# First activations in their own tiles, stored one step sooner; square issued ahead of the subtraction; second output weights kept for two blocks

## Chip, cores and metric

One core of one Trainium2 chip runs the whole program. The metric is device time in microseconds (us) of one execution; the time before is the median of three runs. The parts that matter are TensorE (PE, matrix products; PEld its weight loads), ScalarE (ACT), VectorE (DVE), GpSimd (POOL), SyncE (SP, which here only issues transfers) and the 16 DMA engines.

## The reference

A retention layer, then two MLPs without bias over the same 4608 tokens, all in float32:

```python
ret = (q @ k.T) / 8 * Dmat          # per batch and head, Dmat[i, j] = gamma**(i - j) for i >= j, else 0
x = (ret @ v)                       # heads put side by side: 4608 x 512
h = x @ w_in;  g = h * sigmoid(1.702 * h);  x2 = g @ w_out        # 512 -> 2048 -> 512
h = x2 @ w_in2; g = h - tanh(h);            out = g @ w_out2
```

Each operand of a large product is split into a rounded high part and the rest (two fp32r tiles), and the product is the sum of three passes: high by high, high by low, low by high.

## The kernel before

Tokens lie in 9 blocks of 512 (`NB`), the inner width of 2048 in 16 slices of 128 (`NF`). A **step** s = 16 j + f of the first MLP is `mm_in(s)`: 12 matmuls that give h for block j and slice f, in one PSUM bank. `act_a(s)` makes g from it: ACT takes a tanh into a tile t (L456), DVE makes g in place (L458). `g_store(s)` (L485) sends the tile to DRAM from SP's queue. A **unit** o is the output product of the same numbering: `g_load(o)` brings g back (L504), `act_b(o)` splits it (ACT L509, DVE L510), `wo_load` brings the slice of w_out (L216), and `mm_out` does four parts of 3 matmuls (L526, L528) into four accumulators. After the 16th slice of a block `evac` copies each accumulator to a tile o (ACT L550) and sends it out from ACT's queue (L536).

The order of work on every engine is written out by hand; each engine, and SP's and ACT's transfer queues, go strictly in that order. A tile that is allocated waits until an earlier tile of its tag has been released.

- **Steps 0 to 31** run ahead of all units, beside the retention layer and the decoding of the weights (`dec_a` to `dec_store`, which load raw words L103, use ACT L115, L148 and DVE L113 to L155, and store decoded weights L166, L169).
- **Steps 32 to 79** each carry one unit, o = s - 32 (`LAG`), and every second one a half tile of the retention layer (`attn_step`). Per step SP has in order: the loads of w_out and g for unit o + 2 (`out_loads`), the load of an attention tile, stores of decoded weights, the g store, loads of raw weights. `stores(2)` keeps the two newest steps unstored, so the store issued in step s is that of s - 2. Blocks end with units 15, 31 and 47, in steps 47, 63 and 79.
- **Steps 80 to 143** carry no units (`PAUSE`), but retention until step 126.
- **Tile tags.** `p` has 5 tiles of 128x512: the masked scores of the retention layer (`bat_p`, L326, one in every second step), the t of odd steps, and the four o of an evacuation. `t` has 3 tiles: the t of even steps.
- **The second MLP** starts with one plain block (L677) and goes on with 4 pairs of blocks; for a pair, 7 products of combined operands (`mm_part`, L690) stand for 8, so that a loop step u (32 of them, q = u mod 8) gives four h tiles for `act_2`, between units of the output product. `act_2` does on ACT tanh (L472), square of h (L475), square (L476), relu (L477) and on DVE h - tanh (L474), L479, L480 and a predicated copy (L481). h lies in PSUM in the plain block and in one of four calls per u (L475 with input x); in the other three it lies in SBUF.
- **w_out of the last two blocks** (units 256 to 287): slices 3 to 15 are loaded once each into tiles of the 18 operand tags (`wo_stay`, `xo_tile`, L223), slices 3 to 6 at the end of the last but one u, and 7 to 15 two at a time in the calls of `ready()` in the last u, where the operand tiles become free. Slices 0 to 2 are loaded for each of the two blocks by `wo_load`, like all others.

Of the kernel before, what the change touches and what calls it, by code (L numbers as in the profile page):

```python
# [14 lines left out]
ACTF = mybir.ActivationFunctionType  # L15
# [10 lines left out]
NB = NT // BLK  # L26
KD = DM // P
NF = DFF // P
# [14 lines left out]
PAUSE = 80  # L43
# [5 lines left out]
def kernel(  # L49
# [11 lines left out]
    nc = tc.nc  # L61
# [142 lines left out]
    def wo_load():  # L204
        o = n_w[0]
        n_w[0] += 1
        j, f = divmod(o, NF)
        if j == 0 or j >= 2 * NB or (j >= 2 * NB - 2 and f > 2):
            return
        n_w[1] += 1  # L210
        if second and n_w[1] % 4 == 0:
            t = second["pool"].tile([P, 2, DM], F32R, tag="wos2", name="wos", bufs=1)
        else:
            t = wos_p.tile([P, 2, DM], F32R, tag="wos", name="wos")
        wos[o] = t
        nc.sync.dma_start(out=t.rearrange("p a n -> p (a n)").bitcast(F32), in_=wo_d[int(j >= NB), f])  # L216

    def wo_stay(f):

        if not 2 < f < NF:  # L220
            return
        t = xo_tile()
        nc.sync.dma_start(out=t.rearrange("p a n -> p (a n)").bitcast(F32), in_=wo_d[1, f])  # L223
        for j in (2 * NB - 2, 2 * NB - 1):
            wos[j * NF + f] = t
# [222 lines left out]
    def act_a(s):  # L448

        h = hps.pop(s)  # L450
        if s % 2:
            t = p_p.tile([P, BLK], F32, tag="p", name="t")
        else:
            t = t_p.tile([P, BLK], F32, tag="t", name="t", bufs=3)
        tt[s] = t
        nc.scalar.activation(out=t, in_=h, func=ACTF.Tanh, scale=0.851)  # L456
        copies_out(0)
        nc.vector.scalar_tensor_tensor(out=t, in0=t, scalar=1.0, in1=h, op0=ALU.add, op1=ALU.mult)  # L458
# [3 lines left out]
    def act_2(s, h):  # L462

        tt[s] = t = turn("t")
        sq = t_p.tile([P, BLK], F32, tag="e", name="sq")
        pl = t_p.tile([P, BLK], F32, tag="z", name="pl", bufs=3)
        if not marks:
            marks["t"] = st_p.tile([P, 2, BLK], F32, tag="stg", name="marks", bufs=3)
            marks["n"] = 0
        small = marks["t"][:, marks["n"] % 2]  # L470
        marks["n"] += 1
        nc.scalar.activation(out=t, in_=h, func=ACTF.Tanh)  # L472
        copies_out(0)
        nc.vector.tensor_tensor(out=t, in0=h, in1=t, op=ALU.subtract)  # L474
        nc.scalar.activation(out=sq, in_=h, func=ACTF.Square)  # L475
        nc.scalar.activation(out=pl, in_=sq, func=ACTF.Square, bias=abias)  # L476
        nc.scalar.activation(out=small, in_=sq, func=ACTF.Relu, bias=sbias, scale=-1.0)  # L477

        nc.vector.scalar_tensor_tensor(out=pl, in0=pl, scalar=CB, in1=sq, op0=ALU.add, op1=ALU.mult)  # L479
        nc.vector.scalar_tensor_tensor(out=pl, in0=pl, scalar=C2, in1=h, op0=ALU.mult, op1=ALU.mult)  # L480
        nc.vector.copy_predicated(out=t, mask=small.bitcast(I32), data=pl)  # L481

    def g_store(s):
        gd[s] = dram.tile([P, BLK], F32, tag=f"g{s}", name="gd")
        nc.sync.dma_start(out=gd[s], in_=tt.pop(s))  # L485
# [4 lines left out]
    def turn(what):  # L490

        shape, dt, n = {"t": ([P, BLK], F32, 3), "gl": ([P, BLK], F32, 2), "g": ([P, 2, BLK], F32R, 2)}[what]
        i = turns[what]
        turns[what] += 1
        more = {"t": 3, "gl": 2, "g": 1}[what]
        if second and i % (n + more) >= n:
            return second["pool"].tile(shape, dt, tag=what + "2", name=what, bufs=more)
        if what == "g":
            return g_p.tile(shape, dt, tag="g", name="g")
        return t_p.tile(shape, dt, tag=what, name=what, bufs=n)  # L500
# [31 lines left out]
    def copies_out(keep):  # L532

        while len(copies) > keep:
            dst, o = copies.pop(0)
            nc.scalar.dma_start(out=dst, in_=o)  # L536
# [21 lines left out]
    def out_loads(o):  # L558
        while n_w[0] <= min(o + (3 if second else 2), n_steps - 1):
            wo_load()  # L560
        while n_g[0] <= min(o + (4 if second else 2), n_steps - 1):
            g_load(n_g[0])
            n_g[0] += 1

    def out_split(o):
        while n_b[0] <= min(o + (2 if second else 1), n_steps - 1):
            act_b(n_b[0])
            n_b[0] += 1
# [20 lines left out]
    def xo_tile():  # L589
        tag = xo_tag.pop(0)  # L590
        xo_tag.append(tag)
        if tag == "ws":
            return st_p.tile([P, 2, DM], F32R, tag="ws", name="xo", bufs=2)
        return wts.tile([P, 2, DM], F32R, tag=tag, name="xo")
# [159 lines left out]
    with tc.tile_pool(name="ps_e", bufs=RING - 1, space=bass.MemoryType.PSUM) as ps_e:  # L754
# [11 lines left out]
        for b in range(BPB + 1):  # L766
            if b == 0:
                for bt in range(BPT):
                    at_scale(0, (bt, bt + 1))
                    for i in range(2):  # L770
                        for k in range(2):
                            h = 2 * (2 * bt + k) + i
                            nc.scalar.activation(
                                out=mt_sb[:, bt, i, k], in_=mk_sb, func=ACTF.Copy, scale=jt_sb[:, h:h + 1]
# [51 lines left out]
    def stores(keep):  # L826
        while len(done) > keep:
            g_store(done.pop(0))
# [10 lines left out]
    for s in range(LAG, NB * NF):  # L839
        j, f = divmod(s, NF)  # L840
        o = s - LAG
        if s < PAUSE:
            out_loads(o)
        mm_in(s)
        b = EARLY + BPB + (s - LAG) // 2
        if s % 2 == 0 and b <= TILES * BPT:
            attn_step(b)
            if b == TILES * BPT:
                early_ctx.close()
                second["pool"] = ctx.enter_context(tc.tile_pool(name="second", bufs=1))  # L850
                second["psum"] = ctx.enter_context(tc.tile_pool(name="ps_x", bufs=1, side="right", space=bass.MemoryType.PSUM))
        dec_piece()
        act_a(s)
        if s < PAUSE:
            out_split(o)
        done.append(s)
        stores(2)
        if s < PAUSE:
            some(outs, 4)
        dec_piece(2 if j == 2 else 1)  # L860
        if n_dec[0] >= 3 * (len(chunks) + 2):
            some(prep, 1)
        if j == NB - 1 and f >= 5:
            some(std, 1)
        if j == NB - 1 and f in (8, 11, 14):
            wq_load((f - 8) // 3, True)
# [4 lines left out]
    for i in range(NF):  # L871
        q, half_ = divmod(i, 2)
        s = NB * NF + q + half_ * QS
        h = ps_h.tile([P, BLK], F32, tag="h", name="h")
# [30 lines left out]
    for u in range(pairs * QS):  # L905
        p, q = divmod(u, QS)
        ja = NB + 1 + 2 * p
        a, b = (ja * NF + q, (ja + 1) * NF + q)
        end = p == pairs - 1
        if q == 0:  # L910
            xo.update(new)
            new = {}
            ops = xo_prep(3 + 2 * p, new) if not end else iter(())
        final = q == QS - 1
        stay = iter(range(7, NF)) if end and final else iter(())

        def ready():
            if final:
                some(ops, 1)
                for f in islice(stay, 2):  # L920
                    wo_stay(f)

        n = 4 if final else 3
        x_ps = second["psum"].tile([P, BLK], F32, tag=f"x{u % 2}", name="x")
        y_ps = ps_h.tile([P, BLK], F32, tag="h", name="y")

        mm_part(x_ps, q, 1, True)
        m1 = copied(x_ps, "m1")
        some(outs, n)
        if late:  # L930
            act(*late[0])

        mm_part(y_ps, q, 5, True)
        m5 = copied(y_ps, "m5")
        some(outs, n)
        if late:
            act(*late[1])
        ready()

        mm_part(x_ps, q, 6, False)  # L940
        u2 = copied(x_ps, "u2")
        some(outs, n)
        if u + 1 < pairs * QS:
            wq_load((q + 1) % QS, False)
        ready()

        mm_part(y_ps, q, 3, False)
        h12 = added(y_ps, u2, "h12")
        some(outs, n)
        ready()  # L950

        mm_part(x_ps, q, 7, False)
        h22 = added(x_ps, m5, "h22")
        some(outs, n)
        act(a + QS, h12)
        ready()

        w_ps = second["psum"].tile([P, BLK], F32, tag=f"x{1 - u % 2}", name="w")
        mm_part(w_ps, q, 2, True)
        h11 = added(w_ps, m1, "h11")  # L960
        some(outs, n + final)
        ready()

        mm_part(x_ps, q, 4, False)
        some(outs, 4 + final)
        act(b + QS, h22)
        if not final and q:
            some(ops, 1)
        if end and q == QS - 2:
            for f in range(3, 7):  # L970
                wo_stay(f)
        late = ((a, h11), (b, x_ps))
    for n in late:
        some(outs, 4)
        act(*n)
# [57 lines left out]
```

## Time and profile before

| what | before |
|---|---|
| median of 3 runs (lowest, highest) | 1724.05 us (1722.04, 1724.18) |
| the profiled execution, its own time | 1721.87 us |
| its span, first to last instruction | 1720.1 us |
| PE busy | 1691.1 us (98%) |
| DVE, ACT, POOL busy | 1111.2, 885.1, 113.1 us |
| bytes moved | 497.44 MB, mean 289 GB/s |
| granted TensorE clock, mean | 0.995 of full |

How to read it: PE is busy in nearly all of the span, so its idle time is short and can be listed gap by gap. A gap stands in the timeline in square brackets behind the first instruction after it, with what ended it. The chain of waits follows the last instruction back through what released it. Idle time of the other engines costs nothing unless a PE gap hangs on it. Landing is the time from the issue of a transfer to its end.

### The profile page before, as it was taken

To read this page: it belongs to the slowest core of one execution; us is meant where nothing else is said; L and a number is where in the kernel's file an instruction comes from. 1 tells how busy PE (TensorE), PEld (TensorE's weight loads), DVE (VectorE), ACT (ScalarE), POOL (GpSimd) and SP (SyncE) were. 2 spreads that over 40 slices of the span, in tenths; PEclk is the share of its full clock that TensorE was granted. 3 is DMA by queue.
4 is the path that set the end of the run, shared out by engine and by line. 5 is a ranking of instruction groups with operands and counts; after the bars stand their busy time and mean duration, and the time that the engine had idled before them with its cause. 6 is when DMAs were issued, how large, how long until landed. Compare 5 with 4: busy or idle time off the path is not lost.

```text
span 1720.1 us, 24553 instructions
## 1 busy us (share of the span) xinstructions
PE 1691.1 (98%) x8714; PEld 1383.0 (80%) x8714; DVE 1111.2 (65%) x1806; ACT 885.1 (51%) x1684; POOL 113.1 (7%) x104
## 2 busy tenths in 40 slices
PE   7999999999999999999999999999999999999999
PEld 5788887878877888887888888888888888888777
DVE  6787885656676444457577786677766776666532
ACT  4444442333344433446566576566666665656532
POOL 4011100011002321000000000000000000000000
PEclk9999999999999999999999999999999999999999
DMA  7467779888887777898899899998999999889962
GB/s 265 151 224 248 278 270 317 273 286 281 297 303 275 251 284 250 313 334 293 297 356 315 300 314 332 343 324 278 327 345 315 310 316 310 301 305 327 381 192 86
DMA packets 173866, 497.44 MB, mean 289 GB/s; under 512 B 19632, under 2 KB 20784, under 8 KB 164400
## 3 DMA queue, kind: packets, MB, share of 16 engines
q1 hardware_dynamic: 162800, 476.91, 79.9%
q10 hardware_dynamic: 10944, 18.96, 2.9%
q8 instruction: 69, 1.13, 0.3%
q14 instruction: 53, 0.43, 0.1%
HBM read 363.67 MB, written 132.12 MB: 288 GB/s over the span
## 4 chain that ended last, share of the span: by engine, by line
PE 87%; DMA 5%; DVE 4%; ACT 2%; issue 1%; SPq 0%; ACTq 0%; POOL 0%; DVEq 0%
PE acc L526 21%; PE acc L528 21%; PE h L443 20%; PE x L690 10%; PE y L690 5%; PE w L690 2%; DMA gl<-gd 2%; PE pat L303 2%; PE h L677 2%; DMA x<-o 2%; PE pat L349 1%; PE pat L289 1%; PE pat L318 1%; DVE p L326 1%; DMA at<-in_attn_dram 0%
## 5 line engine op out<-in xcount | busy, mean ns | idle before, releaser
L526 PE MATMUL acc<-g,wos 128*128 128x512 f32 x1536 | 378.0, 394 | 7.3 <-DVE g L510 3.5
L443 PE MATMUL h<-xh,wi 128*128 128x512 f32 x1152 | 374.0, 394 | 2.5 <-ACT xh L363 1.3
L528 PE MATMUL acc<-wos,g 128*128 128x512 f32 x1416 | 344.3, 389 | 3.1 <-DMA wos<-wd 2.5
L526 PEld LDWEIGHTS acc<-g,wos 128*128 128x128 f32 x1536 | 289.3, 189 | 71.8 <-DVE g L510 4.2
L509 ACT ACTIVATE g<-gl 128x512 fp32r<-128x512 f32 x288 | 180.0, 627 | 299.9 <-PE acc L528 150.2
L528 PEld LDWEIGHTS acc<-wos,g 128*128 128x128 f32 x1416 | 265.4, 188 | 59.9 <-ACT marks L477 2.4
L510 DVE TENSOR_TENSOR g<-gl,g 128x512 fp32r<-128x512 f32 x288 | 201.8, 702 | 169.0 <-ACT g L509 167.5
L443 PEld LDWEIGHTS h<-xh,wi 128*128 128x128 f32 x1152 | 216.4, 188 | 53.5 <-issue 5.3
L443 PE MATMUL h<-xl,wi 128*128 128x512 f32 x576 | 224.6, 390 | 0.6 <-DVE xl L364 0.6
L690 PE MATMUL x<-xo,wq 128*128 128x512 f32 x768 | 195.2, 389 | 0.0
L690 PEld LDWEIGHTS x<-xo,wq 128*128 128x128 f32 x768 | 143.9, 188 | 30.8 <-ACT u L896 1.0
L479 DVE SCALAR_TENSOR_TENSOR pl<-pl,sq 128x512 f32<-128x512 f32 x144 | 99.7, 692 | 102.8 <-ACT pl L476 102.4
L458 DVE SCALAR_TENSOR_TENSOR t<-t,h 128x512 f32<-128x512 f32 x144 | 98.4, 685 | 68.4 <-ACT t L456 63.8
L115 ACT ACTIVATE e<-e,ebias 128x512 int32<-128x512 int32 x64 | 46.3, 724 | 180.9 <-DVE e L113 180.9
L443 PEld LDWEIGHTS h<-xl,wi 128*128 128x128 f32 x576 | 108.3, 188 | 23.0 <-DVE xl L364 1.4
L481 DVE COPY_PREDICATED t<-marks,pl 128x512 f32<-128x512 int32 x144 | 109.4, 760 | 15.2 <-ACT xo L597 0.5
L364 DVE TENSOR_TENSOR xl<-pat,xh 128x256 fp32r<-128x256 f32 x61 | 25.8, 423 | 142.0 <-ACT xh L363 139.9
L456 ACT ACTIVATE t<-h 128x512 f32<-128x512 f32 x144 | 84.2, 587 | 50.1 <-PE h L443 49.8
L476 ACT ACTIVATE pl<-sq,abias 128x512 f32<-128x512 f32 x144 | 104.2, 724 | 4.7
L477 ACT ACTIVATE marks<-sq,sbias 128x512 f32<-128x512 f32 x144 | 102.1, 709 | 0.0
L690 PE MATMUL y<-xo,wq 128*128 128x512 f32 x384 | 97.4, 389 | 0.0
L363 ACT ACTIVATE xh<-pat 128x256 fp32r<-128x256 f32 x61 | 23.2, 381 | 136.3 <-PE pat L349 136.3
(89 smaller groups left out, 1957.7 us busy)
## 6 DMA issues: line engine op xcount, KB each, us to landing
wos<-wd SPq DMA_DIRECT2D x246, 512.0 KB, 5.4
gd<-t SPq DMA_DIRECT2D x288, 256.0 KB, 5.4
gl<-gd SPq DMA_DIRECT2D x288, 256.0 KB, 5.2
stg<-in_w_dram SPq DMA_DIRECT2D x64, 512.0 KB, 6.5
at<-in_attn_dram SPq DMA_DIRECT2D x32, 1024.0 KB, 6.0
wq<-wq SPq DMA_DIRECT2D x32, 1024.0 KB, 7.6
wq<-wq SPq DMA_DIRECT2D x32, 768.0 KB, 9.3
wd<-ws SPq DMA_DIRECT2D x32, 512.0 KB, 4.5
```

What stands on the lines that cost most here:

```text
L443: nc.tensor.matmul(h, lhsT=win[f][:, a, k], rhs=xs[b][:, k], start=(n == 0), stop=(n == 3 * KD - 1))
L456: nc.scalar.activation(out=t, in_=h, func=ACTF.Tanh, scale=0.851)
L458: nc.vector.scalar_tensor_tensor(out=t, in0=t, scalar=1.0, in1=h, op0=ALU.add, op1=ALU.mult)
L476: nc.scalar.activation(out=pl, in_=sq, func=ACTF.Square, bias=abias)
L477: nc.scalar.activation(out=small, in_=sq, func=ACTF.Relu, bias=sbias, scale=-1.0)
L479: nc.vector.scalar_tensor_tensor(out=pl, in0=pl, scalar=CB, in1=sq, op0=ALU.add, op1=ALU.mult)
L481: nc.vector.copy_predicated(out=t, mask=small.bitcast(I32), data=pl)
L509: nc.scalar.activation(out=g[:, 0], in_=t, func=ACTF.Copy)
L510: nc.vector.tensor_tensor(out=g[:, 1], in0=t, in1=g[:, 0].bitcast(F32), op=ALU.subtract)
L526: nc.tensor.matmul(acc[m], lhsT=wo[:, a, c], rhs=g[:, b], start=first, stop=last)
L528: nc.tensor.matmul(acc[m], lhsT=g[:, a, c], rhs=wo[:, b], start=first, stop=last)
L690: nc.tensor.matmul(ps, lhsT=wq[q][t][:, o // 2, o % 2 * 2 + k, a], rhs=xo[i][k][:, b], start=first and n == 0, stop=n == 5, skip_group_che ...
```

## The change

In the steps 32 to 84 the t of odd steps comes from the tag `t` like that of even ones, and in steps 32 to 79 only the newest step stays unstored. In `act_2` the square is issued ahead of the subtraction. All 16 slices of the second w_out are loaded once for the last two blocks: slices 0 to 3 at the end of the last but one u, 4 to 15 in the last one, in which `ready()` is called once more.

```diff
@@ wo_load
-        if j == 0 or j >= 2 * NB or (j >= 2 * NB - 2 and f > 2):
+        if j == 0 or j >= 2 * NB - 2:
             return
@@ wo_stay
-        if not 2 < f < NF:
-            return
         t = xo_tile()
@@ act_a
-        if s % 2:
+        if s % 2 and not 2 * NF <= s <= PAUSE + 4:
             t = p_p.tile([P, BLK], F32, tag="p", name="t")
         else:
             t = t_p.tile([P, BLK], F32, tag="t", name="t", bufs=3)
@@ act_2
         nc.scalar.activation(out=t, in_=h, func=ACTF.Tanh)
         copies_out(0)
+        nc.scalar.activation(out=sq, in_=h, func=ACTF.Square)
         nc.vector.tensor_tensor(out=t, in0=h, in1=t, op=ALU.subtract)
-        nc.scalar.activation(out=sq, in_=h, func=ACTF.Square)
@@ steps 32 to 143
-        stores(2)
+        stores(1 if s < PAUSE else 2)
@@ pairs of blocks
-        stay = iter(range(7, NF)) if end and final else iter(())
+        stay = iter(range(4, NF)) if end and final else iter(())
@@ end of a loop step u
         if end and q == QS - 2:
-            for f in range(3, 7):
+            for f in range(4):
                 wo_stay(f)
         late = ((a, h11), (b, x_ps))
+        ready()
```

## Rows read from the trace of the kernel before

**Rows 1.** The page, part 1: busy time, share and instructions of engines.
```profile
PE 1691.1 (98%) x8714; PEld 1383.0 (80%) x8714; DVE 1111.2 (65%) x1806; ACT 885.1 (51%) x1684; POOL 113.1 (7%) x104
```

**Rows 2.** Timeline of PE: start, duration, what, and the gap before it.
```profile
276.81 5.06 PE L526 MATMUL acc<-g,wos 128*128 128x512 f32 x11 [3.17 <-DVE g L510]
...
384.44 0.49 PE L526 MATMUL acc<-g,wos 128*128 128x512 f32 x1 [1.94 <-ACT g L509]
385.25 4.24 PE L526 MATMUL acc<-g,wos 128*128 128x512 f32 x11 [0.31 <-DVE g L510]
...
507.07 0.68 PE L289 MATMUL pat<-at,sbd 128*128 128x128 f32 x4 [0.75 <-DVE s_sb L338]
530.60 0.71 PE L303 MATMUL pat<-at 64*128 64x128 f32 x8 [0.74 <-DVE s_sb L336]
...
781.16 1.66 PE L526 MATMUL acc<-g,wos 128*128 128x512 f32 x6 [1.78 <-ACT o L550]
...
1627.11 3.02 PE L528 MATMUL acc<-wos,g 128*128 128x512 f32 x12 [0.51 <-DMA wos<-wd]
1632.14 3.00 PE L528 MATMUL acc<-wos,g 128*128 128x512 f32 x12 [2.00 <-DMA wos<-wd]
...
1639.82 5.55 PE L528 MATMUL acc<-xo,g 128*128 128x512 f32 x23 [1.01 <-DVE g L510]
```

**Rows 3.** Chain of waits in order of time: start, duration, what.
```profile
261.78 6.53 DMA x<-o
268.47 5.57 DMA x<-o
...
281.87 3.14 PE h L443 x12
...
289.64 2.72 PE h L443 x12
...
480.43 6.98 DMA x<-o
```

**Rows 4.** Timeline of ACT, steps 44, 46, 47 and 83.
```profile
242.78 0.58 ACT L456 ACTIVATE t<-h 128x512 f32<-128x512 f32 x1
...
255.82 0.58 ACT L456 ACTIVATE t<-h 128x512 f32<-128x512 f32 x1
...
268.39 0.60 ACT L550 ACTIVATE o<-acc 128x512 f32<-128x512 f32 x1 [6.16 <-DMA x<-o]
...
500.02 0.59 ACT L456 ACTIVATE t<-h 128x512 f32<-128x512 f32 x1
```

**Rows 5.** Timeline of DVE, step 48.
```profile
274.07 0.69 DVE L326 TENSOR_TENSOR p<-pat,mt_sb 128x512 f32<-128x512 f32 x1 [3.22 <-DMA x<-o]
```

**Rows 6.** Timeline of SP: g stores of steps 47 and 82, late w_out loads.
```profile
263.20 0.32 SPq L485 DMA_DIRECT2D gd<-t  x1
...
495.60 0.43 SPq L485 DMA_DIRECT2D gd<-t  x1
...
1619.48 0.32 SPq L216 DMA_DIRECT2D wos<-wd  x1
...
1625.84 0.32 SPq L216 DMA_DIRECT2D wos<-wd  x1
```

**Rows 7.** Transfers issued in 160 to 480 us: count, KB each, median us to landing.
```profile
gd<-t SPq DMA_DIRECT2D x47, 256.0 KB, 6.2
```

**Rows 8.** Line 485 in the whole run: landing of the g stores.
```profile
DMA to landing us min/median/max: 2.0/5.4/12.8
```

**Rows 9.** Timeline of ACT ahead of the gap at 781 us.
```profile
769.29 0.60 ACT L475 ACTIVATE sq<-h 128x512 f32<-128x512 f32 x1 [3.03 <-DVE t L474]
...
777.10 0.60 ACT L475 ACTIVATE sq<-h 128x512 f32<-128x512 f32 x1 [3.28 <-DVE t L474]
```

**Rows 10.** Waits of the whole run: us in total, times, longest.
```profile
ACT sq L475 <- DVE t L474: 67.0, 47, 3.3
```

**Rows 11.** Transfers in 1596 to 1632 us: packets and bytes.
```profile
DMA packets 5061, 14.48 MB, mean 402 GB/s; under 512 B 561, under 2 KB 561, under 8 KB 5059
```

## Prediction

> **What bounds the kernel now.** I read first the busy times of the page: PE works 1691.1 us [rows 1] of a span of 1720.1 us, so the bound is PE's own stream, and only its 29 us of idle time can be won by moving other work. Next the timeline of PE, searched for gaps: the first 65 us and the last 4 us have gaps that the change does not touch; between them the reader should see a handful of gaps that add up to 12.2 us [rows 2]. Three groups of them belong to steps 48, 64 and 80 onward, that is right behind the evacuations of steps 47, 63 and 79; one stands at 781 us in the plain block of the second MLP; three stand at 1627 to 1640 us, where the last two blocks begin. Then the chain of waits, to see what feeds each gap, and the timelines of ACT, DVE and SP at these places.
>
> At the first evacuation the chain is a store, then a second store [rows 3]. The store of the first o goes out at 261.78 and takes 6.53 us, to 268.31; ACT's copy into the third o starts at 268.39, after 6.16 us of idling [rows 3, 4]. The store of the second o ends at 268.47 + 5.57 = 274.04, and DVE's masked scores start at 274.07 [rows 3, 5]. So the tag p is full: two o tiles, the t of an odd step, one whose store is not yet out, and the scores hold all five. ACT and DVE stand still in turn, the g of the next unit is late, and PE waits 3.17 us. Behind the gap PE pays once more: 11 matmuls take 5.06 us [rows 2], where 12 of the same shape take 2.72 [rows 3], or 0.227 each, so 2.49 for 11; they run at half rate.
>
> **Tile tags and the earlier store (steps 32 to 84).** Removed from p: 24 t tiles that are in it for three steps each. At step 47 p then holds one tile of scores and four free ones, enough for four o tiles; the scores of step 48 take the first o's tile, free at 268.31. They were due about then, since in the undisturbed pair of steps before they follow PE by the same distance, and PE first lacks a g at 276.81 - 3.17 = 273.6 [rows 2], 5.3 us later: cover enough. What goes away:
> - first gap: 3.17 idle [rows 2], 5.06 - 2.49 = 2.57 at half rate, and 3.14 - 2.72 = 0.42 in the next 12 [rows 3]: 6.16 us.
> - second gap: 1.94 + 0.31 idle and 4.24 - 2.49 = 1.75 at half rate [rows 2]: 4.00 us.
> - third: the evacuation of step 79 has the same wait on a store of 6.98 us [rows 3], but PE has free banks there and loses only 0.75 + 0.74 = 1.49 us [rows 2] to a DVE that is late.
>
> Added: each tanh of these steps now waits for a t tile of three, each used every third step. A step is (255.82 - 242.78) / 2 = 6.52 us [rows 4], three are 19.56. The tile of step 46 is taken at 255.82; its store moves to where the one of step 45 stands now, 263.20 [rows 6]; with the median landing of 6.2 [rows 7] it is free after 263.20 - 255.82 + 6.2 = 13.6 us. So 6.0 us are to spare, and without the earlier store, one step of 6.52 later, there would be -0.5: the two edits belong together. If a tanh did wait, ACT's splits of g, its evacuations and its part of the weight decoding queue up behind it, DVE waits for them, and PE for g. On SP the store waits for L458 of one step earlier; behind it stand loads of raw weights and of w_out. The tanh of step 46 starts at 255.82 and DVE follows within 2 us, while the place of its store is 263.20 [rows 4, 6]: some 5 us of cover, so I cost it at nothing; beyond that the price would be SP's delay. About 47 stores of 256 KB move by one step; no bytes are added.
>
> The weak place is steps 80 to 84. There t takes five tiles in five steps, the store goes back to two steps of delay, and steps without units are short. The tile of step 83 is that of step 80, whose store goes out at 495.60 [rows 6]; with a median landing of 5.4 [rows 8] it is free at 501.0, and the tanh of step 83 runs at 500.02 already now [rows 4]. When ACT and DVE come out of step 79 some 3 us earlier, this tanh eats part of it. Bounds for the third gap: all of 1.49 won, or as much lost, if the new wait is as long as the old one; I take 1.0 won, nearer to the gain since DVE's lead is not all eaten.
>
> **Square ahead of subtraction.** In the 48 calls whose h lies in PSUM, the square on ACT now stands behind the subtraction on DVE: 47 waits, 67.0 us [rows 10]. Where DVE is late, these waits pile up on ACT: 3.03 and 3.28 us in the two calls ahead of the gap at 781 us [rows 9], whose releaser is an evacuation copy of ACT, 1.78 us too late for PE [rows 2]. With the square first, ACT runs on, and its 6.31 us are more than three times the gap. I take all of 1.78; bounds 0 and 1.78. The added wait is DVE's: the subtraction now follows the square, 0.6 us of ACT work; behind it on DVE stand L479 and later splits of g, and L479 needs a still later result of ACT anyway. In the pairs of blocks the same waits hide beside a PE without gaps, and are worth nothing. Whichever comes first, one of the two engines waits: the Trainium skill (PSUM — Partial Sum Buffer, PSUM bank collisions raise a hardware error) says that ScalarE and VectorE must not read one bank and quadrant at once, and that a dependency has to keep them apart. The trace agrees (47 waits); by this rule the change turns these waits round, and were DVE's turn as dear as ACT's, the 1.78 would be 0.
>
> **w_out of the last two blocks.** Now slices 1 and 2 are loaded late, at 1619.48 and 1625.84 [rows 6], behind thirteen loads for slices that are needed after them; PE waits 0.51 and 2.00 us for them, and then 1.01 us for the g of slice 4, which ACT and DVE make late [rows 2]. After the change slices 0 to 3 go out in place of 3 to 6, one loop step ahead, into tiles that are long free; 4 to 15 are needed only from 1635 on (slice 4 at 1638 now, less the 2.5 us of waits). Of transfers, six of w_out go and three into operand tiles come, 1.5 MB less; in the crowded stretch itself their number is the same. SP also loses the waits of three w_out loads, ahead of the loads of g. The two waits on w_out (2.51) vanish; whether the g of slice 4 is then later than PE is open, as it hangs on four further ACT and DVE calls: it may cost up to 2 us, or its 1.01 may go too. I take 3.0 won; bounds 1.0 and 3.52. The one more call of `ready()` in earlier loop steps finds its list empty.
>
> **Sum.** 6.16 + 4.00 + 1.0 + 1.78 + 3.0 = 15.9 us. From the profiled execution, 1721.87, that gives 1706.0; from the median of 1724.05, 2.2 us above it, 1708.1. Since late transfers may be what differs between the runs, and these gaps hang on transfers, I take the middle, **1707 us**.
>
> **Rivals.**
> - *The end stays* (the order of loads does nothing): 14.48 MB in 36 us [rows 11] keep the transfers full from 1596 to 1632 us, and the same bytes have to land after the change; then g in place of w_out is late, and the 3.0 are lost: 1707 + 3 = 1710. For it: the loads of g queue in the same crowd. Against it: PE's gaps name w_out, and g is late only behind them. A page's rule goes its way: the Trainium skill (DMA: Bandwidth & Descriptors, Where 436 GB/s comes from) holds that between HBM and SBUF about 358 GB/s per core bind. The row shows 402, so its figure does not hold here; but that a full stretch has one end whatever its order would give these 1710.
> - *Steps 80 to 84 eat their gain and more*: the third gap costs 1.49 more instead of 1.0 less, 1707 + 2.5 = 1709.5. For it: 501.0 against 500.02. Against it: PE has free banks there.
> - *The wait is not the tag's*: ACT's copies wait for something else of the stores, such as the issue of the next one, and the first two gaps stay. Then only 1.0 + 1.78 + 3.0 are won: 1721.87 - 5.8 = 1716, or 1718 from the median. Against it: both starts agree within 0.1 us with the landing of an o store.
> - *Slower: the ring of three t tiles starves.* Place: the tanh of every step from 35 to 79. It costs from a landing of 6.2 + 6.0 = 12.2 us on; at 14 us each step is (14 - 12.2) / 3 = 0.6 longer, 46 steps 27.6, and the time 1721.87 - 15.9 + 27.6 = 1734. It outweighs the gain from a landing of 13.3 us on. Against it: the longest of all 288 stores takes 12.8 [rows 8].
>
> **How the numbers follow.** Forecast 0.70; the end stays 0.12; steps 80 to 84 0.08; not the tag's 0.06; starved 0.02; something without effect on balance 0.02. Low end: all gaps named go, 6.16 + 4.00 + 1.49 + 1.78 + 3.52 = 16.95 from the profiled execution, 1704.9, and some 1.5 less for small waits on ACT and DVE that go along. High end: the two next likely rivals together from the median, 1708.1 + 3 + 2.5 = 1713.6. Range 1703.5 to 1713.5. A measurement of this kernel can tell about 0.2%, 3.4 us, from no change: faster 0.95 (the first four cases, less a little), same 0.03, slower 0.02.
>
> **What would show it.** In the new profile: no gap of PE and no matmuls at half rate at 270 to 290 and 380 to 395 us; no wait of L550 on a store; ACT's square with no wait on L474, and the subtraction waiting on the square instead; no gap at 770; at the end no wait on w_out, and at most one short one on the g of slice 4. Wrong it would be if tanh (L456) waited on g stores outside steps 82 to 84, if p still were full at step 48, or if the gaps at 1600 to 1630 us only changed their releaser.

## The result and the profile after

The changed kernel takes **1705.1 us** (median of 4 runs, 1703.4 to 1706.1), the kernel before 1723.1 (4 runs on the same chip): ratio 0.990, interval 0.988 to 0.992. That is 18 us less; 1707 was predicted, with 1703.5 to 1713.5 as the range. The later comparisons had faster runs of the kernel before (medians of 1719.6 to 1721.9, singles from 1713.7 to 1725.1), and beside one of those (1720.18) the changed kernel, run again, took 1704.58, 15.6 us less. The profiled execution took 1705.08 us, 16.8 less than that of before.

Line numbers behind the edits are smaller by 2: L454 is the tanh, L483 the g store, L502 the g load, L507 and L508 the splits, L524 and L526 the output products, L548 the evacuation; in `act_2` L470 is tanh, L472 the square, L473 the subtraction.

The page of the changed kernel, part 1, to set against [rows 1]:

```profile
PE 1686.0 (99%) x8714; PEld 1382.5 (81%) x8714; DVE 1117.2 (66%) x1806; ACT 884.3 (52%) x1684; POOL 113.8 (7%) x104
```

Span less PE's busy time was 1720.1 - 1691.1 = 29.0 us and is 1703.3 - 1686.0 = 17.3; a further 5.1 us left PE's busy time itself: at the same matmuls (see below) 5.0 us of busy time went behind the first two gaps, where they ran at half rate.

Timeline of PE in the changed kernel (start, duration, what, gap before it): all that is left over 0.2 us between the start and the last microseconds.

```profile
1402.34 0.96 PE L526 MATMUL acc<-wos,g 128*128 128x512 f32 x3 [0.55 <-ACT o L548]
...
1615.52 3.01 PE L526 MATMUL acc<-xo,g 128*128 128x512 f32 x12 [0.28 <-DVE g L508]
1618.89 2.59 PE L526 MATMUL acc<-xo,g 128*128 128x512 f32 x10 [0.35 <-DVE g L508]
1622.60 17.57 PE L526 MATMUL acc<-xo,g 128*128 128x512 f32 x75 [1.12 <-ACT g L507]
```

Of [rows 2] nothing remains at 270 to 530 us and at 781 us; the gap at 1402 was there before with the same 0.55. At the end the gaps name g instead of w_out. The waits on the full tag went with the gaps. ACT's timeline at the first evacuation, then DVE's at step 48, in the changed kernel:

```profile
262.27 1.07 ACT L548 ACTIVATE o<-acc 128x512 f32<-128x512 f32 x2
...
263.28 0.60 ACT L548 ACTIVATE o<-acc 128x512 f32<-128x512 f32 x1
...
263.90 0.60 ACT L548 ACTIVATE o<-acc 128x512 f32<-128x512 f32 x1
```

```profile
270.43 0.69 DVE L324 TENSOR_TENSOR p<-pat,mt_sb 128x512 f32<-128x512 f32 x1
```

The four copies run one after the other, where the third had idled 6.16 us [rows 4], and the masked scores start with no idling at all, where they had waited 3.22 us [rows 5].

Waits of the whole run in the changed kernel (us in total, times, longest us):

```profile
DVE pl L477 <- ACT pl L474: 33.3, 63, 1.3
...
DVE t L473 <- ACT sq L472: 13.2, 15, 2.4
...
ACT t L454 <- DMA gd<-t: 2.3, 1, 2.3
```

The 47 waits and 67.0 us of [rows 10] are gone, and what came in their place is 15 waits of DVE with 13.2 us. The last row is the price of the new ring: one tanh in the whole run waits for a g store. The chain of waits of the changed kernel names that store:

```profile
483.81 6.99 DMA gd<-t
```

It ends at 483.81 + 6.99 = 490.80, and the tanh of step 83 starts at 490.88; the store is that of step 80.

To find where the time went, I also took the difference of both traces at the same matmul, counted from the start (my own working from the starts of PE's instructions). Before minus after: -1.1 us at the start, +6.14 over the first gap, +4.29 over the second, +1.83 over the third, +2.11 at 781 us, +0.66 between 800 and 1600 us (0.33 at 1306 and 0.27 at 1357), +2.39 from 1600 us on; 16.5 at the last matmul, with 0.2 in smaller pieces. The same working for the other profiles is used below. The 0.33 at 1306 us is in nearly every one of them, with and without the square's new place, and so belongs to the profile of before; the 0.27 at 1357 us is in all seven that have the square first and in no other.

### The profile page after: what moved, and what is told of

It is laid out like the page before. It is cut to its first block, busy times and chain, and to the rows that moved or that the text cites. A ratio compares the mean times of both kernels' runs of the same rounds, so it can differ in the third digit from the quotient of the medians.

```text
span 1703.3 us, 24579 instructions
## 1 busy us (share of the span) xinstructions
PE 1686.0 (99%) x8714; PEld 1382.5 (81%) x8714; DVE 1117.2 (66%) x1806; ACT 884.3 (52%) x1684; POOL 113.8 (7%) x104
## 4 chain that ended last, share of the span: by engine, by line
PE 93%; DMA 3%; DVE 2%; ACT 1%; issue 0%; SPq 0%; POOL 0%; ACTq 0%
PE acc L524 23%; PE h L441 22%; PE acc L526 21%; PE x L688 10%; PE y L688 5%; PE h L675 3%; PE w L688 2%; PE pat L301 2%; PE pat L347 1%; PE pat L287 1%; PE pat L316 1%; DMA wos<-wd 1%; DMA gl<-gd 1%; DMA gd<-t 1%; DMA at<-in_attn_dram 0%; DVE p L324 0%
## 5 line engine op out<-in xcount | busy, mean ns | idle before, releaser
L524 PE MATMUL acc<-g,wos 128*128 128x512 f32 x1536 | 373.0, 391 | 0.0
L507 ACT ACTIVATE g<-gl 128x512 fp32r<-128x512 f32 x288 | 180.9, 628 | 354.6 <-PE acc L526 166.0
L524 PEld LDWEIGHTS acc<-g,wos 128*128 128x128 f32 x1536 | 287.0, 188 | 61.9 <-issue 2.4
L526 PE MATMUL acc<-wos,g 128*128 128x512 f32 x1344 | 326.8, 389 | 0.6 <-ACT o L548 0.6
L508 DVE TENSOR_TENSOR g<-gl,g 128x512 fp32r<-128x512 f32 x288 | 200.0, 695 | 192.6 <-ACT g L507 190.4
L526 PEld LDWEIGHTS acc<-wos,g 128*128 128x128 f32 x1344 | 252.2, 188 | 53.3 <-ACT o L548 1.0
L477 DVE SCALAR_TENSOR_TENSOR pl<-pl,sq 128x512 f32<-128x512 f32 x144 | 99.5, 691 | 35.5 <-ACT pl L474 33.3
L454 ACT ACTIVATE t<-h 128x512 f32<-128x512 f32 x144 | 84.1, 587 | 54.0 <-PE h L441 49.3
```

Source lines behind the costliest of these rows:

```text
L507: nc.scalar.activation(out=g[:, 0], in_=t, func=ACTF.Copy)
L508: nc.vector.tensor_tensor(out=g[:, 1], in0=t, in1=g[:, 0].bitcast(F32), op=ALU.subtract)
L524: nc.tensor.matmul(acc[m], lhsT=wo[:, a, c], rhs=g[:, b], start=first, stop=last)
L526: nc.tensor.matmul(acc[m], lhsT=g[:, a, c], rhs=wo[:, b], start=first, stop=last)
```

## The experiments

Times are medians, and each is set against the runs of the kernel before of its own comparison.

### The tag and the sooner store, without the rest

```diff
-        if s % 2:
+        if s % 2 and not 2 * NF <= s <= PAUSE + 4:
...
-        stores(2)
+        stores(1 if s < PAUSE else 2)
```

> The kernel before with the first activations of steps 32 to 84 in their own tag and the store one step sooner, nothing else. Theory (tag p was full at each evacuation): the first two gaps and the half rate behind them go (6.16 and 4.00 us), and the third (1.49), so 11.6 us less than before, ratio 0.993; the gaps at 781 us (1.78) and at the end (3.5) stay. Rival (the copies wait for something else of the stores): ACT's copy L550 still waits 6 us on a store, and the time is that of before within 2 us.

Measured: 1708.27 against 1720.13, ratio 0.993 (0.992 to 0.995), 11.9 us less. No PE gap over 0.2 us at 255 to 500 us, no wait of an evacuation on a store of o. The gap at 768 us (1.06) and those at the end stay. Around 510 us are two gaps, 0.50 and 0.70: the second stands ahead of the same matmul as the gap at 530.60 in [rows 2], so this half of the third gap stays, and the first is new. Two thirds or more of the whole gain are these two edits.

> The tile tag and the sooner store together, without the other edits, once more and in more rounds. Questions: what do the two edits win together, 11.9 us as in the first look (1708.27 against 1720.13)? And do the two gaps at 508 and 517 us (0.50 + 0.70) belong to this kernel? Up to 660 us its instructions are those of the changed kernel, which shows no gap there. If they belong to the run, they are gone or elsewhere in this profile; if they come again at the same place and size, something in the order of the code sets them. Theory: they belong to the run; the gain is 10 to 12 us.

Measured: 1708.36 against 1721.90, ratio 0.992 (0.990 to 0.993), 13.5 us less. That is above the 10 to 12 expected. The gap at 508 us is gone, the one at 517, the second half of the third gap, is there again with 0.72: the theory held for one of the two.

### The tag alone, the store two steps behind

```diff
-        stores(1 if s < PAUSE else 2)
+        stores(2)
```

> The new tag for the first activations, but the store left two steps behind. Theory (a t tile is held from its tanh to the landing of its store, 13.6 us with the sooner store and some 20 us without, against 19.6 us for three steps): nearly every second tanh of steps 35 to 79 waits on a store, by 0 to 3 us, and PE gets new gaps in units; half or more of the 11.6 us is lost again, 1714 to 1722 us. Rival (the sooner store is not needed, since ACT's waits hide): as with both edits, 11.6 us less than before.

Measured: 1712.48, ratio 0.996 (0.994 to 0.998), 7.7 us less. In its waits:

```profile
ACT t L456 <- DMA gd<-t: 32.0, 15, 3.8
```

and in PE's timeline, behind the first two evacuations:

```profile
272.55 2.79 PE L526 MATMUL acc<-g,wos 128*128 128x512 f32 x11 [0.81 <-DVE g L510]
...
376.17 2.81 PE L526 MATMUL acc<-g,wos 128*128 128x512 f32 x11 [0.31 <-DVE g L510]
```

The wait of the tanhs is there as expected, but in 15 of the 53, and most of it hides: some 4 us of the gain are lost. The theory was right in kind and too dear.

### The sooner store alone, t still in p

```diff
-        if s % 2 and not 2 * NF <= s <= PAUSE + 4:
+        if s % 2:
```

> The store one step sooner alone, odd activations still in tag p. Theory (p is full at an evacuation with the t of that step and the scores in it, whether the t of two steps before is out or not): at step 47 one tile more is free in time, so the third copy no longer waits 6.2 us, but the scores of step 48 still wait for the first or second o to land: one of the two waits is left, and 4 to 9 of the 11.6 us are won. Rival (the late store alone was the cause): all 11.6 us are won.

Measured: 1711.98, ratio 0.995 (0.994 to 0.997), 8.1 us less. The size was hit, the reason was not. ACT's timeline at the first evacuation, DVE's and PE's:

```profile
263.15 0.60 ACT L550 ACTIVATE o<-acc 128x512 f32<-128x512 f32 x1 [1.45 <-DMA gd<-t]
...
268.72 0.60 ACT L550 ACTIVATE o<-acc 128x512 f32<-128x512 f32 x1 [4.97 <-DMA x<-o]
```

```profile
270.57 0.68 DVE L326 TENSOR_TENSOR p<-pat,mt_sb 128x512 f32<-128x512 f32 x1
```

```profile
269.37 0.97 PE L526 MATMUL acc<-g,wos 128*128 128x512 f32 x3 [0.24 <-ACT o L550]
```

ACT still idles 4.97 us for a store of o, nearly as long as in [rows 4], and PE loses 0.24 instead of 3.17. What is gone is DVE's wait, the 3.22 of [rows 5]. So of the two engines that stood still in turn it was DVE, through the split of g behind the scores, that PE hung on; ACT's wait alone is covered.

> The sooner store without the tile tag once more, beside the run above on the same chip. Question: does the store alone win about all of what the two edits win? Behind the start its first profile is only 0.5 us longer than that of the two edits (1646.1 against 1645.6), while the medians were 3.7 us apart (1711.98 against 1708.27). Theory by the profiles: within 1.5 us of the run above. Rival by the medians: 3 to 5 us slower than it, with gaps behind the first or second evacuation that its first profile did not show.

Measured: 1712.12 against 1721.90, ratio 0.994 (0.993 to 0.995): 9.8 us less, and 3.8 behind the two edits beside it, as in the first pair (3.7). The rival was right. It has gaps at 270, 378, 498 and 521 us (0.31 + 0.30 + 0.32 + 0.69), where the two edits have one of 0.72, and a gap of 0.72 on an evacuation copy at 1616 us, which they do not have. At the same matmuls the two profiles differ by 0.9, 1.0 and 0.8 us over the three evacuations and by 0.65 at the end, with nothing on balance between; a start later by 1.8 us makes up the rest of the 5.05 us between these two executions. So in this pair the store alone leaves up to 1 us at each evacuation that the tag takes away.

### Steps 80 to 84: where the tag ends, and where the store changes

The odd t of steps 81 and 83 back into p:

```diff
-        if s % 2 and not 2 * NF <= s <= PAUSE + 4:
+        if s % 2 and not 2 * NF <= s < PAUSE:
```

> The changed kernel, but odd activations use their own tag up to step 79 only, not to 84. Theory (steps 81 and 83 would take tiles of p that the four copies of step 79 hold until their stores land): a wait on those stores comes back at steps 80 to 84, and up to the third gap's 1.5 us; time of the changed kernel plus 0 to 2 us. Rival (the tanh of steps 82 to 84 that waits for a g store is the dearer one): 0 to 2 us faster than the changed kernel.

Measured: 1704.00, ratio 0.991 (0.989 to 0.992). The sooner store kept up to step 84 instead:

```diff
-        stores(1 if s < PAUSE else 2)
+        stores(1 if s < PAUSE + 5 else 2)
```

> The changed kernel with the sooner store up to step 84 instead of 79. Theory (the tanh of steps 82 to 84 waits 2.3 us on a g store, beside a PE that runs ahead with free banks): that wait goes, and the time is that of the changed kernel within 0.5 us. Rival (the wait is on the path): 1 to 2 us faster than the changed kernel.

Measured: 1704.39, ratio 0.990 (0.989 to 0.992). In both no tanh waits for a g store, and PE has no gap over 0.2 us at 490 to 535 us; the wait on stores of o that was expected of the first did not come back either. The changed kernel, run again on the chip of the last comparison, shows the other side:

> The changed kernel once more, unedited, beside the one above on the same chip. Question: how far do two profiles of the same kernel differ? The gaps at the end should come out at 1.5 to 2.0 us again, no gap over 0.3 us at 270 to 290 and 380 to 395 us, and the time at 1702 to 1707; if the end's gaps move by over 0.5 us between two profiles of the same kernel, then differences of that size between the kernels at the end say nothing. Rival for the start: the first product behind the start comes at 64.7 us in the changed kernel and at 63.6 in the kernel before; if that belongs to the kernel, it comes at 64.7 again, and if it belongs to the run, anywhere between 61 and 66.

Measured: 1704.58, ratio 0.992 (0.989 to 0.994). Its wait, and PE's timeline:

```profile
ACT t L454 <- DMA gd<-t: 2.7, 1, 2.7
```

```profile
509.77 0.46 PE L287 MATMUL pat<-at,sbd 128*128 128x128 f32 x2 [0.28 <-DVE p L324]
...
518.33 0.72 PE L301 MATMUL pat<-at 64*128 64x128 f32 x8 [0.74 <-DVE s_sb L334]
```

My expectation of no gap held for 270 to 400 us, and I had not thought of these. The second of them is again the second half of the third gap. Six profiles have one tanh that waits for a g store in these steps (the changed kernel twice, the two edits without the rest twice, and the two kernels on the end below), 2.3 to 3.2 us, and gaps that add up to 0, 1.02, 1.20, 0.72, 0.37 and 0.41 us at 508 to 518 us; the two edited kernels of this section have no such wait, and no gap. At the same matmuls 0.5 to 1.8 us of the third gap are won with the wait, and 2.0 in both profiles without it. This points to the new wait as what eats into the gain, by an amount that changes from run to run; it is an agreement of eight profiles, and no run parts it from other causes. The times of these kernels (1704.0 to 1705.1) are too near to each other to rank them.

### The square ahead of the subtraction, alone

```diff
+        nc.scalar.activation(out=sq, in_=h, func=ACTF.Square)
         nc.vector.tensor_tensor(out=t, in0=h, in1=t, op=ALU.subtract)
-        nc.scalar.activation(out=sq, in_=h, func=ACTF.Square)
```

> The kernel before with the square ahead of the subtraction, nothing else. Theory (the square's waits on DVE pile up on ACT only where DVE is late): the gap at 781 us (1.78 us) goes, and short waits of PE on ACT in the pairs of blocks get fewer (up to 1 us); the 67.0 us of ACT's waits become some 15 to 30 us of DVE's; 1.8 to 2.8 us less than before. Rival (the waits only change sides): the gap stays, no change in time.

Measured: 1715.31 against 1719.57, ratio 0.998 (0.997 to 0.999), 4.3 us less, with an interval of 1.5 to 5.7. The gap at 781 us is gone. That gap is 0.89 to 1.78 us in the seven profiles with the subtraction first, and is in none of the seven with the square first. At the end the last gap of [rows 2] is gone too, with one of 0.22 us ahead of it:

```profile
1618.89 3.02 PE L528 MATMUL acc<-wos,g 128*128 128x512 f32 x12 [0.56 <-DMA wos<-wd]
...
1623.78 4.57 PE L528 MATMUL acc<-wos,g 128*128 128x512 f32 x12 [1.87 <-DMA wos<-wd]
```

2.43 us are left there, where before had 0.51 + 2.00 + 0.22 + 1.01 = 3.74 (the 0.22 at 1638 us). But this need not be the square's doing. The 12 matmuls behind the second gap take 4.57 us here, where before had 3.00, and the granted clock behind the gap has fallen:

```profile
1622.00:1627.00 5.00, 3.22 (x8) 2.58 (x9) 3.50 (x6) 2.42 (x5) 0.00 (x0) 0.70 0.95 339
```

(stretch, its length, busy time of PE, PEld, DVE, ACT and POOL, then the granted clock, 0.70, the DMA share and GB/s). In before it is 1.00 at 1632 to 1637 us. A slower PE comes later to the g of slice 4, and finds it there. The second profile of the tag and the sooner store, which keeps the subtraction first, shows the same:

```profile
1618.22 4.57 PE L528 MATMUL acc<-wos,g 128*128 128x512 f32 x12 [2.06 <-DMA wos<-wd]
```

Its first profile has the clock at 1.00 behind a gap of 2.02 us, and keeps the gaps of 0.23 and 1.01. At the same matmuls the square alone wins 0.64 us from 1600 us on, not 1.31, and the five profiles with neither the square first nor the slices -0.75 to 0.26.

### The w_out slices alone

> The kernel before with all 16 slices of the second w_out kept for the last two blocks, nothing else. Theory (the loads of slices 1 and 2 were late because of their place in SP's order): no wait on w_out at the end, the g of slices 3 to 5 late by 1.5 to 2 us in all; 2 us less than before. Rival (the stretch is full of transfers, so the order does not matter): the waits only change their releaser, no change in time.

Measured: 1719.28 against 1719.57, ratio 0.999 (0.998 to 1.001): not to be told from no change. Its gaps at the end:

```profile
1629.06 1.20 PE L526 MATMUL acc<-xo,g 128*128 128x512 f32 x4 [0.33 <-DVE g L508]
...
1632.68 0.73 PE L526 MATMUL acc<-xo,g 128*128 128x512 f32 x2 [1.06 <-ACT g L507]
1633.92 16.43 PE L526 MATMUL acc<-xo,g 128*128 128x512 f32 x64 [0.51 <-DVE g L508]
```

No wait on w_out, and 1.90 us of waits on g in place of 3.74. So 1.84 us of gaps are gone, but the clock has fallen behind those that are left:

```profile
1632.00:1637.00 5.00, 3.81 (x10) 2.72 (x11) 3.15 (x5) 1.89 (x3) 0.00 (x0) 0.75 0.74 279
```

and PE gives most of it back: at the same matmuls 0.62 us are won from 1600 us on, in this one profile, which agrees with the times.

### Why g is late at the end: ACT's work, or the loads?

The two last calls of `act_2` moved apart, so that ACT has room for the splits:

```diff
-    for n in late:
-        some(outs, 4)
-        act(*n)
     some(outs, 4)
+    act(*late[0])
+    some(outs, 4)
     stores(0)
+    some(outs, 8)
+    act(*late[1])
+    some(outs, 4)
+    stores(0)
```

> The changed kernel with the last activation of h in PSUM moved behind two more units of the output product, the stores of the earlier ones sent before them. Theory (the last gaps, 0.28, 0.35 and 1.12 us, are ACT and DVE giving the last activations ahead of the splits of g): the gaps shrink to under 0.6 us in all, 1.2 us faster than the changed kernel. Rival (the loads of g are what is late there): the gaps stay and only change their releaser.

Measured: 1704.44, ratio 0.990 (0.988 to 0.993), as the changed kernel. ACT's split in its timeline:

```profile
1620.54 0.63 ACT L507 ACTIVATE g<-gl 128x512 fp32r<-128x512 f32 x1 [5.01 <-DMA gl<-gd]
```

ACT is free 5.01 us ahead and waits for the load; PE keeps 0.34 + 1.12 there. So it is the loads. The changed kernel itself has such a wait, 2.84 us at 1621.91. Why the loads are late is a further question. The next run puts slices 14 and 15 of w_out behind them:

```diff
         late = ((a, h11), (b, x_ps))
-        ready()
     for n in late:
         some(outs, 4)
         act(*n)
+    ready()
```

> The changed kernel, with the last two w_out slices (14 and 15) loaded behind the last three loads of g instead of ahead of them. Question: is the g that is still late at 1615 to 1623 us late because these two loads of 256 KB each stand ahead of it? Theory: yes in part; SP has them at 1614.87, 0.9 us ahead of the first of the three loads of g, and they share the transfer engines with it. So the waits of ACT's split on a load of g (2.84 us at 1621.91) shrink to under 2 us, and PE's three gaps there (0.28 + 0.35 + 1.12 = 1.75) to 0.5 to 1.0; the time 1704 to 1705, which the times alone cannot tell from the changed kernel. Rival: the earlier loads of w_out that still fill the transfers, or the stores of g that come first, make the loads late; then the gaps stay at 1.5 to 2.0.

Measured: 1703.19 (1702.9 to 1703.8), ratio 0.991 (0.989 to 0.993); the changed kernel beside it has 1704.58. The two slices are of 512 KB each, not of 256 KB as the expectation has it. SP's timeline, then ACT's, then PE's:

```profile
1613.85 0.37 SPq L502 DMA_DIRECT2D gl<-gd  x1
1614.28 0.49 SPq L483 DMA_DIRECT2D gd<-t  x1
1614.86 0.91 SPq L221 DMA_DIRECT2D xo<-wd  x2
1615.87 0.38 SPq L502 DMA_DIRECT2D gl<-gd  x1
```

```profile
1618.10 0.63 ACT L507 ACTIVATE g<-gl 128x512 fp32r<-128x512 f32 x1 [0.67 <-DMA gl<-gd]
1623.49 0.63 ACT L507 ACTIVATE g<-gl 128x512 fp32r<-128x512 f32 x1 [4.76 <-DMA gl<-gd]
```

```profile
1616.76 3.03 PE L526 MATMUL acc<-xo,g 128*128 128x512 f32 x12 [0.34 <-DVE g L508]
1620.12 8.04 PE L526 MATMUL acc<-xo,g 128*128 128x512 f32 x34 [0.32 <-DVE g L508]
1629.04 11.22 PE L526 MATMUL acc<-xo,g 128*128 128x512 f32 x47 [0.88 <-ACT g L507]
```

The wait fell as the theory had it, but the gaps stayed at the rival's 1.5 to 2.0. The wait of 2.84 us is down to 0.67, and the gap that it made at 1622 us is gone; but the slices did not get behind all the loads of g, the load after them is late in its turn (4.76), and PE pays 0.88 for that one. The sum of the gaps is 1.54 instead of 1.75 and, in the second profile of the changed kernel, 1.62: the lateness has moved on. It is the fastest kernel of the study, but by 1.4 us with four runs each, which is less than what the start differs between runs (below); and from 1600 us on it wins 2.2 us at the same matmuls, where the four profiles with the changed kernel's order of work there win 2.4 to 2.9. One cause stays open. In the changed kernel SP stands still for 3.6 us ahead of the g store at 1614.45, by the profile until a store of ACT's queue has landed, and loads of g stand behind it:

```profile
SPq L483 <- DMA out_dram<-o: 3.6, 1, 3.6
```

No run here parts this from the fullness of the transfers.

## Why the prediction was right, step by step

**Tile tags and the earlier store.** Forecast 6.16 + 4.00 + 1.0 = 11.2; the trace gives 6.14 + 4.29 + 1.83 = 12.3 at the same matmuls, the times of the two edits without the rest 11.9 and 13.5. The mechanism, a full tag behind the evacuation, is what the profile after shows. Three points in it were less exact than the sum (and of the t of odd steps 26, not 24, leave p up to step 84).
- *Which wait decides.* The text let ACT and DVE stand still in turn. The sooner store alone shows that DVE's wait is the one that PE feels.
- *"The two edits belong together."* That was too strong. The tag alone keeps 7.7 of 11.9 us, the store alone 8.1 of 11.9 and, run again, 9.8 of 13.5. The working of 13.6 us against 19.56 held in kind: in the changed kernel the store at that place goes out at 265.88, 8.94 us after the tanh at 256.94, and with the landing of 6.2 [rows 7] the tile is held for 15.1 us. No tanh waits in steps 32 to 79. What failed is that I counted the wait (-0.5 us to spare) and did not price it: of 32.0 us of such waits in the kernel with the tag alone some 4 reached the time.
- *Steps 80 to 84.* The wait of this rival is real: the tanh of step 83 waits for the store of step 80, as told. Its price was bounded by 1.49 won and 1.49 lost; the six profiles with the wait win 0.5 to 1.8 us at the same matmuls, around the 1.0 taken.

**The half rate.** The terms 2.57 and 1.75 came from one profile, where the granted clock, after PE had stood still in the first two gaps, is 0.57 and 0.66 in the stretches behind them (1.00 is the upper level, 2.4 GHz; a mean between is part of the stretch at the lower, 1.2 GHz):

```profile
275.00:283.00 8.00, 6.19 (x15) 4.87 (x16) 5.62 (x10) 1.72 (x3) 0.00 (x0) 0.57 0.91 266
...
385.00:390.00 5.00, 4.75 (x14) 3.79 (x15) 3.96 (x8) 1.11 (x2) 0.00 (x0) 0.66 0.59 210
```

(columns as above). In the kernel with the w_out edit alone, which changes nothing up to there, it is 0.79 and 1.00:

```profile
275.00:283.00 8.00, 7.03 (x24) 5.68 (x25) 4.77 (x9) 1.73 (x3) 0.00 (x0) 0.79 0.89 271
...
383.00:388.00 5.00, 4.69 (x20) 3.68 (x20) 4.29 (x8) 1.44 (x3) 0.00 (x0) 1.00 0.63 207
```

Its gaps are 3.17 and 1.73 + 0.31 us, and 11 matmuls take 4.38 and 2.79 instead of 5.06 and 4.24. That is (5.06 + 4.24) - (4.38 + 2.79) = 2.1 us less for the same work, so the two terms are a property of the run as much as of the kernel. The kernel with the square alone has 0.79 and 1.00 as well, with 4.28 and 2.80 us for 11 matmuls. The scatter of the runs of before, over 11 us where those of the changed kernel keep within 3, goes with the clock too: of the 48 runs of before in the later comparisons, the nine with a mean granted clock of 0.991 to 0.993 took 1720.8 to 1725.1 us (median 1723.8), the nine with 0.997 to 0.999 took 1713.7 to 1719.6 (median 1716.3).

The size of the terms was worked out across two measures: 2.49 for 11 matmuls goes by the chain, the 5.06 and 4.24 by the timeline, in which 11 at the full rate take 2.79 (the tag alone, above). That makes each term 0.30 smaller; at the same matmuls all that was won beside the idle time is 2.97 and 2.04, against 2.99 (2.57 + 0.42) and 1.75 forecast.

**Square ahead of subtraction.** The term was 1.78, with bounds of 0 and 1.78. At its place 2.11 us were won against the profile of before; the other six profiles with the subtraction first have a smaller gap there (0.89 to 1.62), so the term is about right and the profile of before lay at its upper end. The time of the edit alone, 4.3 us, is more, but its interval, 1.5 to 5.7, holds the 1.78. "In the pairs of blocks the same waits [...] are worth nothing" was nearly so: between 800 and 1600 us, 0.27 us at 1357 us is all that only the profiles with the square first show. The fear that DVE's turn would be as dear as ACT's did not come true. The Trainium skill (PSUM — Partial Sum Buffer, PSUM bank collisions raise a hardware error) has the two engines kept apart at one bank and quadrant; the trace agrees that one waits for the other, but says that the order matters: 47 waits and 67.0 us with DVE first, 15 and 13.2 with ACT first, and DVE's waits on ACT at its next step fell from 102.4 us in 112 waits to 33.3 in 63.

**w_out: mis-sized.** The term was 3.0 with bounds of 1.0 and 3.52. The gaps at the end went from 3.74 to 1.75, 1.99 less, and at the same matmuls 2.39 us are won from 1600 us on. How much of this is the slices' own is not settled: alone the slices won 0.62 and the square 0.64, each in one profile with the clock fallen behind a gap, and together 2.2 to 2.9 in six profiles, in which the clock stays at 1.00 there. The step that failed is the open one: I let the wait on the g of slice 4 go with the rest, and loads of g are late in its place; three gaps are left, where the prediction would have had at most a short one. The rival "the end stays" was half right, and the last kernel shows how: what one load gains in this stretch, the next one pays. The transfers of the 36 us up to 1618 us in the changed kernel:

```profile
DMA packets 5036, 14.16 MB, mean 393 GB/s; under 512 B 560, under 2 KB 560, under 8 KB 5034
```

That is 14.16 MB where [rows 11] have 14.48: the stretch is as full as before.

**The sum.** Forecast 1706.0 for the profiled execution, measured 1705.1. It is that near since errors cancel: tags +1.1, square +0.3 at its place, pieces between 800 and 1600 us +0.7, the end -0.6 (2.39 against 3.0), a later start -1.1, small pieces +0.2, and 0.3 behind the last matmul, which add up to the 0.9 of difference. That it came so near is luck in part: a start 1 us earlier or later, as runs have it, moves it as much.

**The other rivals.** "The wait is not the tag's" fell: the copies run without idling. "The ring starves" fell for the changed kernel; the tag without the sooner store is the nearest to it, and even there 32.0 us of waits of the tanhs cost some 4.

## What to carry to other kernels

When several engines wait for one full pool of tiles, find the one whose wait the bound engine feels, by a run that frees one of them; here, freeing one tile sooner won over two thirds of what moving all of them did. Where two engines read one bank in turn, try the order in which they come to it: here the later one's turn was then cheap (13.2 us of waits in place of 67.0). A gap that has left the list need not be time won: look at the granted clock behind the gaps ahead of it, and compare two profiles at the same matmul. At the end 1.31 and 1.84 us of gaps went with one edit each, and only 0.64 and 0.62 us were won.

## What the runs showed of the chip that was not expected

The start differs between runs by more than most terms of the sum. The first long product of the kernel, behind a gap of 1.20 us on a weight that DVE decodes, comes at 63.61 us in the profile of before, at 64.72 in that of the changed kernel, at 62.82 in its second profile, and anywhere from 61.24 to 65.29 in the fourteen profiles, though no edit touches anything ahead of it. That is 4 us of 1705, and it is in every one of these times; to compare two profiles it has to be subtracted first. Why it moves was not looked into. The granted clock is another thing that a kernel does not settle: in two profiles of the tag and the sooner store, behind gaps of 2.02 and 2.06 us ahead of the same 12 matmuls, it stays at 1.00 in one and falls to 0.73 in the other.
